# More expert matmuls ahead of a routing round's first comparison sums, from the third round on

## The chip, the cores and the metric

One core of a Trainium2 chip runs one program. The metric is the device time of that core in microseconds: 834.33 us before, the median of three runs (832.85 to 835.11).

## The reference

Attention over 4 x 8 heads of 576 positions feeds a dense layer pair, and that feeds a mixture of eight experts, in which tokens are assigned greedily, by falling logit, each expert taking at most 288 of 2304:

```python
x = attn_out ...                       # (2304, 512)
g = np.maximum(h, 0) + alpha * np.minimum(h, 0)   # h = x @ w_in
x = g @ w_out                          # (2304, 512)
logits = x @ w_gate                    # (2304, 8)
for idx in np.argsort(-logits.flatten()):
    tok, e = idx // 8, idx % 8
    if assigned[tok] >= 0 or counts[e] >= 288: continue
    assigned[tok] = e; counts[e] += 1
for e in range(8):
    out[mask_e] = np.maximum(x[mask_e] @ w1[e], 0) @ w2[e]
```

## The kernel before

The first 560 us are attention and the dense layers. The change concerns what follows: the routing and the eight experts, which run side by side.

**Routing.** It goes in eight rounds, p = 0 to 7; each finds the expert that fills up first, its 288 tokens, and closes it. In a round, DVE writes the best free expert of each token (`best`, L796 to L801), and `search` then brackets the threshold in four iterations (five in round 0). An iteration is a comparison on DVE (`against`, L912, two halves, tile `cmp`), 18 short matmuls on TensorE that sum it (L1088, tile `prt`; "the sums" below), a test on DVE (L1094, tile `ge`), two more short matmuls (L1097, L1098; "the step" below), and a new set of thresholds on DVE (L1100). Then `members` (two matmuls, L1165 and L1166, and DVE work) numbers the tokens, and `index` makes the list `ix` of their rows (18 matmuls, L1212, and DVE L1215). Round 7 has no search. POOL's queue gathers the rows (L1231, tile `xg`), and TensorE transposes them (L1266, `expert_x`), which ACT and DVE split into `exh` (L1270) and `exl` (L1271).

**An expert.** Expert p (the one that round p found) has 96 matmuls of the first layer (L1300, eight blocks f, 12 each, into `phx`), then 96 of the second (L1318, four columns c, 24 each, into `pyx`). After block f, ACT writes `hh` (L1306) and DVE `hl` (L1307); the second layer needs both of every block. ACT empties a column into `yt` (L1324), TensorE transposes it back after the next expert's first block (L1336), ACT writes `row` (L1344) and POOL's queue scatters it (L1347). A weight block is loaded by SP's queue (`wr`, L1243, three buffers), cast by ACT in two halves (`ws`, L1248), and its rest is taken by POOL in two subtractions (L1251), behind the gather of the same expert. There are two sets of `ws`, so the weights of expert p+1 are prepared while expert p runs.

**What sets the order.** TensorE's order is written out by a planner (the loop at the end of the kernel): `experts()` yields the expert's pieces with a cost in ns each (490 for four first-layer matmuls, 370 for three second-layer ones), `routing()` yields the delay until its next TensorE piece may stand in the order. When the planner's time `now` reaches `ready`, the routing piece is placed, else the next expert piece. `ahead(now)` places the gather and the weights of a round that has been numbered. The delay before an iteration's sums is `(LB if it == 0 else LU) + NB * K / 1.92` with LB = 1700. The other engines' order follows from the program order and a scheduler, and each engine runs its queue in order. So ACT, DVE and POOL each carry both routing and expert work in one line.

Of the kernel before, what the change touches and what calls it, by code (L numbers as in the profile page):

```python
# [25 lines left out]

LEAST = 896 * 16
KG = 15
FW = 20
ND, OG0, OGS, OG1 = 11, 48, 2, 125.5  # L30
WE = 1
# [16 lines left out]
LB, LU, LG, LM, LI, LX, LX1, L0 = 1700, 600, 400, 4300, 5600, 8000, 3000, 0  # L48
# [57 lines left out]
def attention_moe_kernel(ctx, tc, qt, kt, vt, wm, alpha, wg, we, out, NB=18, dbg=None):  # L106
# [81 lines left out]
    def w_scales():  # L188
# [19 lines left out]
        nc.vector.tensor_tensor(s[:, 0:1], to[:, 0:1], to[:, 2:], ALU.mult)  # L208
        nc.vector.tensor_scalar(s[:, 2:], back[:, 0:1], back[:, 1:2], 2.0 ** KG, op0=ALU.mult, op1=ALU.mult)
        nc.vector.tensor_tensor(s[:, 2:], s[:, 2:], e[:, 2:], ALU.mult)  # L210
# [50 lines left out]
    def small_loads():  # L261
# [8 lines left out]
        for a, b in zip(slope[0], scaled):  # L270
            nc.vector.tensor_scalar(b, a, 2.0 ** -KG, None, op0=ALU.mult)

# [414 lines left out]
    def fill(n):  # L687

        for _ in range(min(n, len(rest))):
            with tc.issue_after(LAST["pl"].ins):  # L690
                rest.pop(0)()
# [214 lines left out]
    def rows_of(ap):  # L906
        return ap[:, :, None].to_broadcast([P, ap.shape[1], J])

    def against(out, ramp, x, op):

        d = [P, out.shape[1], ramp.shape[1] // J, J]
        nc.vector.tensor_tensor(out.rearrange("p b (k j) -> p b k j", j=J),  # L912
                                ramp.rearrange("p (k j) -> p k j", j=J)[:, None].to_broadcast(d),
                                x[:, :, None, :].to_broadcast(d), op)
# [70 lines left out]
    def do(fn, *a):  # L985
        if LABEL is not None:
            LABEL.append((nc.get_next_instruction_name(), fn.__name__, [x for x in a if isinstance(x, int)]))
        fn(*a)
# [60 lines left out]
    def warm(n):  # L1049

        for _ in range(n):
            nc.tensor.matmul(idle[:, :2 * P], ones, ones[:, None, :].to_broadcast([P, 2, P]), start=True, stop=True)
# [5 lines left out]
    def search(p, scale):  # L1058

        r = R[p]  # L1060
        K, its, KL = (K1, I1, KL1) if p else (K0, I0, KL0)

        u16 = rt.tile([P, NB, J], F16, name="u16", bufs=3)
        nc.vector.tensor_scalar(u16, rows_of(r["m"]), scale[K], MID, op0=ALU.mult, op1=ALU.add)
        old = r["m"], scale[K], ALU.mult
        for it in range(its):
            last = it == its - 1
            if last:
                K = KL
            th = ramps["steps"][:, 64 - K // 2:64 + K // 2]  # L1070
            for cs in HALVES:
                against(cmp[:, cs, :K], th, u16[:, cs], ALU.is_le)
            if not last:

                by = K if it < its - 2 else KL // 2
                u, uk = u_, uk_[it % 2]
                nc.vector.tensor_scalar(u, old[0], old[1], 2.0 * K, op0=old[2], op1=ALU.min)
                nc.vector.tensor_scalar(uk, u, -2.0 * K, float(by), op0=ALU.max, op1=ALU.mult)
            if not p:
                fill(FILL[2 + it])  # L1080
            elif p == 1 and it == 0:
                warm(WP)

            yield (LB if it == 0 else LU) + NB * K / 1.92
            pr = psum.tile([P, 2, NE], F32, name="prt", bufs=PR)
            cnt, ne = pr[:, 0], pr[:, 1]
            for c in range(NB):
                nc.tensor.matmul(cnt, cmp[:, c], r["ob"][:, c], start=c == 0, stop=c == NB - 1)  # L1088
            if not p:
                fill(FG_)  # L1090
            ge = rt.tile([P, NE], F16, name="ge", bufs=2)
            if not last:
                g1 = rt.tile([P, 1], F16, name="g1", bufs=2)
                nc.vector.tensor_scalar(ge[:K], cnt[:K], float(CAP), None, op0=ALU.is_ge, op1=ALU.max,  # L1094
                                        accum_out=g1[:K])
                yield LG
                nc.tensor.matmul(ne[:, :1], times[by][:K], half[:K], start=True, stop=False)  # L1097
                nc.tensor.matmul(ne[:, :1], times[by][:K], g1[:K], start=False, stop=True)  # L1098
                u16 = rt.tile([P, NB, J], F16, name="u16", bufs=3)
                nc.vector.tensor_scalar(u16, rows_of(uk), ne[:, :1], MID, op0=ALU.subtract, op1=ALU.add)  # L1100

                ne_ = rt.tile([P, 1], F32, name="ne", bufs=2)
                nc.vector.tensor_copy(ne_, ne[:, :1])
                old = uk, ne_, ALU.subtract
            else:
                nc.vector.tensor_scalar(ge[:K], cnt[:K], float(CAP), None, op0=ALU.is_ge)
                yield LG
                nc.tensor.matmul(ne, ones[:K], ge[:K], start=True, stop=True)
                n = rt.tile([P, 1], F32, name="n", bufs=2)
                nc.vector.tensor_reduce(n, ne, axis=AX.X, op=ALU.max)  # L1110

                v = v_
                nc.vector.tensor_scalar(v, u16[:, :, 0], n, MID - K // 2, op0=ALU.subtract, op1=ALU.subtract)
        ev_ = rt.tile([P, NE], F32, name="ev", bufs=2)
        nc.vector.scalar_tensor_tensor(ev_, ne, 8.0, e_rev, op0=ALU.mult, op1=ALU.add)
        r["u"], r["pick"] = v, ev_
# [69 lines left out]
    def index(p):  # L1186
# [30 lines left out]
        if not p:  # L1217
            warm(FW)

# [150 lines left out]
    def routing():  # L1370
        for p in range(NE):
            for d in routing_(p):
                yield d * M1 if p == 1 else d
# [27 lines left out]
    def experts():  # L1401
        for _ in stepped(("expert_x", 0), (1 for _ in expert_x_(0))):
            yield 0, XC
        yield 0, 400
        for p in range(NE):
            for f in range(8):
                for c in stepped(("expert_1", p), (1 for _ in expert_1(p, f))):
                    yield 0, 490
                yield 0, 490
                if p > 1 and f == YF:  # L1410
                    for k in range(G3):
                        do(expert_y, p - 1, k)
                        yield 0, 450
            for c in range(4):
                if 0 < p < NE - 1 and c == XE:
                    while p + 1 not in gathered:
                        yield None, 0
                    yield gathered[p + 1], 1300
                    do(expert_x, p + 1)
                for _ in stepped(("expert_2", p), (1 for _ in expert_2(p, c))):  # L1420
                    yield 0, 370
                yield 0, 370
            if p == 0:
                while 1 not in gathered:
                    yield None, 0
                yield gathered[1], 1300
                do(expert_x, 1)
                for k in range(G3):
                    do(expert_y, 0, k)
                    yield 0, 450  # L1430
            current[0] = min(p + 1, NE - 1)
            if p == NE - 1:
                for k, half in (0, 0), (1, 0), (0, 1), (2, 0), (1, 1), (2, 1):
                    do(expert_y, p, k, half)

    def ahead(now):

        for p in sorted(placed - set(gathered)):
            if p <= current[0] + 1:
                with tc.high_priority(offset=HP):  # L1440
                    do(gather, p)
                gathered[p] = now + (LX if p > 1 else LX1)
        for p in sorted(picked):
            while loaded[p] < (8 if p in gathered else W0 if p else 0) and p <= current[0] + 1:
                do(expert_weights, p, loaded[p])
                loaded[p] += 1

    current = [0]
    route, work = routing(), experts()
# [3 lines left out]
    now = gathered[0] = LX1  # L1453
# [6 lines left out]
    w = next(work, None)  # L1460
    while w is not None or ready < INF:
        if ready <= now and len(placed) <= current[0] + 2 or w is None or w[0] is None:
            now = max(now, ready)
            with tc.high_priority(offset=HP):
                d = next(route, None)
            ready = INF if d is None else now + d
        elif w[0] <= now or ready == INF or len(placed) > current[0] + 2:
            now = max(now, w[0]) + w[1]
            w = next(work, None)
        else:  # L1470
            now = min(w[0], ready)
        ahead(now)
# [46 lines left out]
```

## Time and profile before

| | us |
|---|---|
| median of three runs | 834.33 |
| the profiled execution | 840.6 |
| its span, first to last instruction | 838.9 |
| busy: TensorE, DVE, ACT, POOL | 796.7, 578.8, 458.0, 281.5 |
| mean granted TensorE clock | 0.969 |

TensorE is busy for 95% of the span. The share says little by itself, because a matmul at the lower clock is longer and counts as busy too. The stretches to look at are those of single experts, from the first matmul of an expert to that of the next, with the clock of each and the waits inside it.

### The profile page before, as it was taken

The page shows a single profiled execution, that of the slowest core. Times are in us where ns is not written, and L with a number is a line of the kernel's source. Part 1 is how long each engine was busy: PE and PEld are TensorE (multiplying, and loading weights), DVE is VectorE, ACT ScalarE, POOL GpSimd, SP SyncE. Part 2 cuts the span into 40 slices and gives each one's busy share as a digit, 9 for nine tenths or more (in the row PEclk, how much of TensorE's full clock was granted, in tenths as well). Part 3 has the DMA queues.
Part 4 walks back from the last instruction along what each step waited for, and adds up shares of the span by engine and source line. Part 5 has one row for each costly group of instructions (what it writes and reads, how often), then busy time and mean ns, then how long its engine had stood idle before and what let it go on. Part 6 is the DMA issues. An engine that isn't in the chain of part 4 may idle for free.

```text
span 838.9 us, 18221 instructions
## 1 busy us (share of the span) xinstructions
PE 796.7 (95%) x6854; PEld 647.0 (77%) x6854; DVE 578.8 (69%) x1757; ACT 458.0 (55%) x1105; POOL 281.5 (34%) x256
## 2 busy tenths in 40 slices
PE   7789999999999999999999999989999979999996
PEld 5567776777777767777777777758999879999995
DVE  6996588988687777888868754786776666752120
ACT  4899367856555655655655544424546344455531
POOL 4344020101110010101100000019799875888921
PEclk7799999999999999999999999998999899999999
DMA  8997101114233142242411000034656554566500
GB/s 295 297 343 232 38 26 51 39 29 112 63 102 77 32 115 57 64 102 64 106 34 31 9 1 27 2 111 148 202 185 203 155 179 155 157 182 199 162 29 29
DMA packets 49144, 93.22 MB, mean 111 GB/s; under 512 B 22800, under 2 KB 22816, under 8 KB 49056
## 3 DMA queue, kind: packets, MB, share of 16 engines
q1 hardware_dynamic: 45984, 82.62, 33.1%
q0 software_dynamic: 3072, 9.44, 3.6%
q8 instruction: 54, 0.88, 0.4%
q14 instruction: 34, 0.28, 0.1%
HBM read 78.40 MB, written 9.44 MB: 105 GB/s over the span
## 4 chain that ended last, share of the span: by engine, by line
PE 80%; DVE 7%; DMA 5%; ACT 2%; issue 2%; POOL 1%; SPq 1%; another core or an unknown queue 0%; POOLq 0%; DVEq 0%; ACTq 0%
PE ph L705 22%; PE py L748 18%; PE pyx L1318 12%; PE phx L1300 11%; PE S L535 3%; PE py L740 2%; PE prt L1088 2%; PE pav L629 2%; DMA raw<-in_wm_dram 2%; PE pav L621 1%; PE pt L570 1%; DMA wr<-in_we_dram 1%; DVE wf L184 1%; PE pty L879 1%; PE pt L650 1%
## 5 line engine op out<-in xcount | busy, mean ns | idle before, releaser
L705 PE MATMUL ph<-xh,wp 128*128 128x256 f16 x1536 | 199.1, 273 | 0.3 <-DVE g L712 0.3
L705 PEld LDWEIGHTS <-wp 128*128 128x128 f16 x1536 | 147.6, 98 | 42.2 <-issue 1.6
L1251 POOL TENSOR_TENSOR ws<-wr,ws 128x512 fp32r<-128x512 f32 x128 | 160.4, 1287 | 13.7 <-ACT ws L1248 13.3
L436 POOL TENSOR_TENSOR ks<-kr,ks 64x512 fp32r<-64x512 f32 x34 | 51.2, 1511 | 282.3 <-ACT ks L435 271.0
L748 PE MATMUL py<-wp,gh 128*128 128x512 f16 x468 | 131.0, 380 | 0.3 <-ACT gh L730 0.3
L711 ACT ACTIVATE g<-ph,sg 128x256 f32<-128x256 f32 x144 | 67.5, 470 | 95.9 <-PE ph L705 94.7
L1318 PE MATMUL pyx<-hh,ws 128*128 128x288 f32 x512 | 111.0, 303 | 0.0
L1248 ACT ACTIVATE ws<-wr 128x512 fp32r<-128x512 f32 x128 | 73.2, 627 | 55.8 <-DMA wr<-in_we_dram 49.3
L712 DVE SCALAR_TENSOR_TENSOR g<-ph,sa,g 128x256 f32<-128x256 f32 x144 | 68.9, 478 | 42.7 <-ACT g L711 42.3
L1300 PE MATMUL phx<-exh,ws 128*128 128x288 f32 x512 | 88.2, 310 | 0.0
L1318 PEld LDWEIGHTS pyx<-hh,ws 128*128 128x128 f32 x512 | 85.5, 191 | 0.0
L748 PE MATMUL py<-wp,gl 128*128 128x512 f16 x234 | 78.2, 380 | 0.7 <-DVE gl L731 0.6
L1300 PEld LDWEIGHTS phx<-exh,ws 128*128 128x128 f32 x512 | 76.0, 197 | 0.8 <-ACT exh L1270 0.3
L1318 PE MATMUL pyx<-hl,ws 128*128 128x288 f32 x256 | 76.2, 298 | 0.0
L730 ACT ACTIVATE gh<-g 128x256 f16<-128x256 f32 x117 | 48.4, 413 | 44.6 <-DVE g L712 39.4
L748 PEld LDWEIGHTS <-gh 128*128 128x128 f16 x468 | 44.0, 98 | 31.4 <-issue 0.5
L1307 DVE SCALAR_TENSOR_TENSOR hl<-phx,hh 128x288 fp32r<-128x288 f32 x64 | 28.8, 455 | 52.6 <-ACT hh L1306 52.1
L731 DVE TENSOR_TENSOR gl<-g,gh 128x256 f16<-128x256 f32 x117 | 53.0, 453 | 15.6 <-ACT gh L730 15.4
L561 ACT ACTIVATE e<-e,mn 128x128 f32<-128x128 f32 x116 | 45.2, 392 | 11.0 <-DVE mn L558 10.8
L1318 PEld LDWEIGHTS pyx<-hl,ws 128*128 128x128 f32 x256 | 48.9, 191 | 0.0
L1300 PE MATMUL phx<-exl,ws 128*128 128x288 f32 x256 | 47.3, 308 | 0.0
L1306 ACT ACTIVATE hh<-phx 128x288 fp32r<-128x288 f32 x64 | 25.1, 404 | 39.2 <-PE phx L1300 27.2
(302 smaller groups left out, 1541.1 us busy)
## 6 DMA issues: line engine op xcount, KB each, us to landing
wr<-in_we_dram SPq DMA_DIRECT2D x64, 512.0 KB, 3.7
raw<-in_wm_dram SPq DMA_DIRECT2D x16, 1023.8 KB, 6.3
kr<-in_k_dram SPq DMA_DIRECT2D x68, 128.0 KB, 2.7
qr<-in_q_dram SPq DMA_DIRECT2D x64, 128.0 KB, 2.7
y_dram<-y SPq DMA_DIRECT2D x16, 256.0 KB, 2.0
vr<-in_v_dram SPq DMA_DIRECT2D x13, 256.0 KB, 2.6
whole<-in_v_dram SPq DMA_DIRECT2D x4, 256.0 KB, 6.6
whole<-in_q_dram SPq DMA_DIRECT2D x4, 128.0 KB, 2.5
```

The lines of the kernel that those rows point to most:

```text
L436: nc.gpsimd.tensor_sub(ks[64:], KR[n][64:], f32(ks[64:]))
L561: nc.scalar.activation(e[:, h], e[:, h], AF.Exp, bias=mn[:, h:h + 1], scale=-1.0, accum_out=SM[b][:, hh:hh + 1])
L705: LAST["l1"] = nc.tensor.matmul(ph, w[f][:, c * P:(c + 1) * P], x[u][:, c, :], start=i == 0, stop=i == 4 * len(pairs) - 1)
L711: KEPT[order.index((u, f))] = nc.scalar.activation(g, ph, AF.Copy, scale=sg)
L712: TURN[order.index((u, f))] = nc.vector.scalar_tensor_tensor(g, ph, sa, g, op0=ALU.mult, op1=ALU.max)
L730: nc.scalar.activation(gh, g, AF.Copy)
L731: nc.vector.tensor_sub(gl, g, gh)
L748: nc.tensor.matmul(PY[u][i], a[:, i * P:(i + 1) * P], w[f][:, 512:], start=f == 0 and j == 0, stop=f == FT - 1 and j == 2)
L1248: nc.scalar.activation(wh[s][:, h], w[:, h], AF.Copy)
L1251: (nc.vector if on_dve else nc.gpsimd).tensor_sub(wl[s][:, h], w[:, h], f32(wh[s][:, h]))
L1300: nc.tensor.matmul(ph, w[s][:, c * P:(c + 1) * P], x[:, c], start=i == 0, stop=i == 11)
L1318: nc.tensor.matmul(py, w[s][:, cs], r[x][f], start=i == 0, stop=i == 23)
```

## The change

The delay before the sums of a round's first iteration grows by DB = 2500 ns of the planner's time in rounds 2 to 7 (round 7 has no search). A second edit lets the expert work go on as soon as a gather is placed that it waited for in the planner; nothing else differs.

```diff
+DB = 2500
@@ search
-            yield (LB if it == 0 else LU) + NB * K / 1.92
+            yield (LB if it == 0 else LU) + NB * K / 1.92 + (DB if p > 1 and it == 0 else 0)
@@ planner loop, after a routing piece
             ready = INF if d is None else now + d
+            if w is not None and w[0] is None:
+                ahead(now)
+                w = next(work, None)
```

Lines behind the first edit move by one (L1088 is L1089 after), those behind the last by four.

TensorE, round 4, between the index matmuls of round 3 (L1212, tile `g`) and the sums of the first comparison (tile `cmp`). Before:

```order
L1212 LDWEIGHTS g
L1212 MATMUL prt<-col,g 128x6
L1300 MATMUL phx<-exl,ws_8833 128x288 x4
L1300 MATMUL phx<-exh,ws_8833 128x288 x4
L1300 MATMUL phx<-exh,ws_8840 128x288 x4
L1300 MATMUL phx<-exl,ws_8840 128x288 x4
L1300 MATMUL phx<-exh,ws_8840 128x288 x4
L1300 MATMUL phx<-exh,ws_8847 128x288 x4
L1088 LDWEIGHTS cmp
L1088 MATMUL prt<-ob,cmp 128x8
```

After, the last rows ahead of the same sums:

```order
L1319 MATMUL pyx<-hh_9314,ws_8858 128x288
L1319 MATMUL pyx<-hl_9315,ws_8858 128x288
L1319 MATMUL pyx<-hh_9314,ws_8858 128x288
L1319 MATMUL pyx<-hh_9331,ws_8865 128x288
L1319 MATMUL pyx<-hl_9332,ws_8865 128x288
L1319 MATMUL pyx<-hh_9331,ws_8865 128x288
L1089 LDWEIGHTS cmp
L1089 MATMUL prt<-ob,cmp 128x8
```

Before, 24 expert matmuls stood there, all of expert 2's first layer; now 45 stand there, all of its second layer. Rounds 2 and 3 go from 24 to 45 as well, round 5 from 24 to 44, round 6 from 23 and 12 transposes to 45; each round thus ends later in the expert work than before.

DVE, round 3, from the thresholds after the first step to the second test (`ge`). Before, `exl` of expert 2 stood an iteration later:

```order
L1100 TENSOR_SCALAR u_8923<-rs,prt 128x72
L1103 COPY ne<-prt 128x1
L912 TENSOR_TENSOR cmp<-rs,u_8923 128x1280
L912 TENSOR_TENSOR cmp<-rs,u_8923 128x1024
L1077 TENSOR_SCALAR rs<-rs,ne 128x18
L1078 TENSOR_SCALAR rs<-rs 128x18
L1094 TENSOR_SCALAR ge,g_8968<-prt 128x8
```

After:

```order
L1101 TENSOR_SCALAR u_8967<-rs,prt 128x72
L1104 COPY ne<-prt 128x1
L913 TENSOR_TENSOR cmp<-rs,u_8967 128x1280
L913 TENSOR_TENSOR cmp<-rs,u_8967 128x1024
L1272 TENSOR_TENSOR exl<-ptx,exh 128x288 x4
L1078 TENSOR_SCALAR rs<-rs,ne 128x18
L1095 TENSOR_SCALAR ge,g_9025<-prt 128x8
```

The four `exl` of the next expert now stand ahead of a test, in rounds 2, 3 and 4 alike.

ACT, first layer of expert 2 from its fourth block on (`ws` are the weights of expert 3). Before:

```order
L1306 ACTIVATE hh_9263<-phx 128x288
L1248 ACTIVATE ws_9323<-wr 128x512 x2
L1306 ACTIVATE hh_9280<-phx 128x288
L1306 ACTIVATE hh_9385<-phx 128x288
L1306 ACTIVATE hh_9402<-phx 128x288
L1248 ACTIVATE ws_9330<-wr 128x512 x2
L1306 ACTIVATE hh_9451<-phx 128x288
```

After:

```order
L1307 ACTIVATE hh_9237<-phx 128x288
L1307 ACTIVATE hh_9280<-phx 128x288
L1249 ACTIVATE ws_9190<-wr 128x512 x2
L1307 ACTIVATE hh_9297<-phx 128x288
L1249 ACTIVATE ws_9366<-wr 128x512 x2
L1307 ACTIVATE hh_9314<-phx 128x288
L1249 ACTIVATE ws_9373<-wr 128x512 x2
L1307 ACTIVATE hh_9331<-phx 128x288
```

The third weight block of expert 3 was cast ahead of the fifth `hh`; now it is cast ahead of the last. In experts 3 and 4 even the fourth block of the next weights stands ahead of the last `hh`.

## Rows read from the trace of the kernel before

**Rows 1.** Stages, TensorE: stretch, us, busy (instructions), granted clock, DMA share, GB/s

```profile
638.26:674.47 36.21, 34.45 (x317) 0.91 0.52 158
674.47:713.79 39.32, 35.03 (x337) 0.91 0.54 173
713.79:745.80 32.01, 31.53 (x318) 1.00 0.60 175
...
774.48:802.49 28.01, 28.01 (x218) 1.00 0.43 130
```

**Rows 2.** Waits of TensorE, 560 to 838 us: total us, times, longest

```profile
PE prt L1088 <- DVE cmp L912: 5.2, 3, 3.5
PE prt L1097 <- DVE ge L1094: 2.3, 3, 1.2
```

**Rows 3.** Timeline, TensorE: start, us, work, [idle before, releaser]

```profile
653.54 0.41 PE L1088 MATMUL prt<-ob,cmp 128*128 128x8 f16 x10 [1.54 <-DVE cmp L912]
...
686.87 0.41 PE L1088 MATMUL prt<-ob,cmp 128*128 128x8 f16 x10 [3.45 <-DVE cmp L912]
```

**Rows 4.** Stages: us, PE, PEld, DVE, ACT, POOL busy, granted clock, DMA

```profile
653.00:661.00 8.00, 7.24 (x61) 6.80 (x62) 4.50 (x16) 1.56 (x3) 7.67 (x8) 0.57 0.52 144
```

**Rows 5.** Chain of waits: start, us, what; expert matmuls at either clock

```profile
657.07 2.88 PE pyx L1318 x12
...
816.60 12.67 PE pyx L1318 x96
```

**Rows 6.** Chain of waits, up to the first wait of rows 3

```profile
643.50 5.34 DMA wr<-in_we_dram
...
649.99 0.40 ACT hh L1306
...
650.41 0.46 DVE hl L1307
...
652.75 0.74 DVE cmp L912
```

**Rows 7.** Timeline, ACT, ahead of the second wait

```profile
680.99 0.41 ACT L1306 ACTIVATE hh<-phx 128x288 fp32r<-128x288 f32 x1
685.18 0.41 ACT L1306 ACTIVATE hh<-phx 128x288 fp32r<-128x288 f32 x1 [3.78 <-remote]
```

**Rows 8.** Timeline, DVE: a later comparison, and three `exl`

```profile
635.01 1.26 DVE L1271 TENSOR_TENSOR exl<-ptx,exh 128x288 fp32r<-128x288 f32 x3
...
661.99 1.42 DVE L912 TENSOR_TENSOR cmp<-rs,u 128x1280 f16<-128x1280 f16 x2
```

**Rows 9.** Timeline, TensorE: a step, the sums after it, the transposes of gathered rows

```profile
661.42 0.18 PE L1097 MATMUL prt<-half,times 128*128 128x1 f16 x1
...
663.53 0.61 PE L1088 MATMUL prt<-ob,cmp 128*128 128x8 f16 x18
...
670.09 1.15 PE L1266 MATMUL ptx<-ident,xg 96*128 96x96 f32 x12
671.03 0.38 PE L1318 MATMUL pyx<-hh,ws 128*128 128x288 f32 x1
```

**Rows 10.** Timeline, TensorE: two shorter waits

```profile
239.80 0.20 PE L629 MATMUL pav<-vp,et 128*128 128x64 f16 x1 [0.96 <-DVE et L608]
...
567.14 0.16 PE L1097 MATMUL prt<-half,times 128*128 128x1 f16 x1 [1.25 <-DVE ge L1094]
```

**Rows 11.** Stages, TensorE: the clock behind those two

```profile
240.00:242.00 2.00, 1.58 (x28) 1.00 0.00 0
...
570.00:575.00 5.00, 4.98 (x35) 0.50 0.65 198
```

**Rows 12.** Timeline, ACT: a cast that waits for its load

```profile
653.71 1.15 ACT L1248 ACTIVATE ws<-wr 128x512 fp32r<-128x512 f32 x2 [1.79 <-DMA wr<-in_we_dram]
```

**Rows 13.** The tile `wr`, 600 to 760 us: POOL's subtraction (ns); load time

```profile
L1251 POOL TENSOR_TENSOR ws<-wr,ws x86: 1262/1286/1317, 598.8 to 759.9; 128x512 fp32r<-128x512 f32 x86
...
DMA to landing us min/median/max: 3.6/3.7/5.1
```

**Rows 14.** Timeline, POOL and TensorE: last gather issue of expert 0, first use

```profile
566.04 0.92 POOL L1231 DMA_INDIRECT xg<-y_dram,ix  x1 [0.30 <-issue]
...
569.25 0.90 PE L1284 MATMUL ptx<-ident,xg 96*128 96x96 f32 x4 [0.30 <-DMA xg<-y_dram,ix]
```

## Prediction

> **What bounds the kernel now.** I read the stages first, cut at the first matmul of each expert. Expert 6 has no routing beside it and takes 28.01 us at full clock; expert 4, with four sums, a `members` and an `index`, takes 32.01 us, also at full clock. Experts 2 and 3 carry about the same routing and take 36.21 and 39.32 us, at a mean clock of 0.91 [rows 1]. So TensorE sets the pace here, and the two slow experts are where something can be had. Expert 2 has one `members` more than expert 4 (0.1 us) and expert 3 one `index` more (0.5 us, about what 18 such short matmuls take). What they lose is 36.21 - 32.01 - 0.1 = 4.1 us and 39.32 - 32.01 - 0.5 = 6.8 us, together **10.9 us**.
>
> The waits of TensorE say at what: 5.2 us in three waits for a comparison, and less for tests [rows 2]. The timeline puts two of the three, 5.0 us, at 653.5 us (1.54 us, round 4) and 686.9 us (3.45 us, round 5), both at the first comparison of a round [rows 3], where the change puts more work. The rest of the loss is the clock: 0.57 granted over the 8 us from 653 [rows 4], which is (1 - 0.57) / 0.5 x 8 = 6.9 us at 1.2 instead of 2.4 GHz. An expert matmul goes at 2.88 / 12 = 0.24 us there and at 12.67 / 96 = 0.132 us at full clock [rows 5]. A stretch after a wait thus costs 4.1 - 1.5 = 2.6 us by the span of expert 2, and 6.9 x (1 - 0.132 / 0.24) = 3.1 us by the pitch of the matmuls; I use 2.6.
>
> The chain of waits tells why the comparison was late. A weight load took 5.34 us, the cast behind it waited, `hh` stood behind the cast on ACT, `hl` behind `hh`, and the comparison behind `hl` on DVE [rows 6]. For the second wait the same `hl` and comparison stood behind an `hh` that started 3.78 us after ACT was free, and the profile names no engine that released it [rows 7].
>
> **What the change removes.** Between the `members` matmuls of a round and the next round's first sums, 72 expert matmuls and the `index` stood in round 4, and 92 stand now: 20 x 0.132 = 2.6 us more, where DVE was 1.5 us late. In round 5 it was 61 matmuls and 12 transposes (1.2 us), and it is 92: 31 x 0.132 - 1.2 = 2.9 us more, where DVE was 3.5 us late. By count alone wait one goes and 0.6 us of wait two stays. But in round 4 the comparison no longer has the late `hh` near it: the last block of the first layer is three matmuls ahead of the `index`, and 45 matmuls follow. In round 5 the last `hl` stands ahead of the comparison, yet 36 matmuls (4.8 us) lie between its block and the sums. I take both waits and both clock stretches as gone: **-10.9 us**. Rounds 2, 3 and 6 had no wait there beyond the 0.2 us left over in [rows 2], and gain nothing. The added work is no new work: the same matmuls stand elsewhere later, and as TensorE has work of the experts to the end, the later rounds cost nothing by themselves. The second edit of the planner moves no row by itself, since the expert work never has to ask for rows not yet gathered.
>
> **What it adds.** Three places.
>
> First, the test behind the four `exl` in rounds 2, 3 and 4. From a step on, DVE's comparison ends after 661.99 + 1.42 - 661.42 = 2.0 us; four `exl` take 4 x 1.26 / 3 = 1.7 us at most [rows 8], less their overlap, say 1.5, and the test 0.25: 3.75 us. TensorE does in that time, in round 3, transposes (0.94 us), three matmuls (0.4), the sums (some 0.5, since the next start overlaps their end) and six matmuls (0.8) [rows 5, 9], 2.65 us. It waits 1.1 us; in round 2 the transposes of `yt` give the same sum, 1.1 us; in round 4 six matmuls more stand there, 0.8 us, and 0.3 us is left. Sum **+2.5 us**; bounds: 0, if `exl` finds a gap earlier, and 3.5.
>
> Second, the last `hh` and `hl` of experts 3 and 4. ACT has the cast of the fourth weight block of the next expert ahead of the last `hh`. That load needs a `wr` buffer, which POOL frees after the first block's two subtractions (2 x 1.29 us), and the load takes 3.7 us, at most 5.1 [rows 13]. The first block's cast stands behind the fourth `hh` (the third in expert 4), so the fourth cast ends about 1.2 + 2.6 + 3.7 + 1.2 = 8.7 us behind that, while four blocks and an `index` take 4 x 1.6 + 0.5 = 6.9 us on TensorE (five blocks in expert 4). The last `hh` is then 1.8 us late in expert 3 and in time in expert 4. The second layer wants the last `hl` 21 matmuls (2.8 us) behind its block, of which `hh` and `hl` take 1.2 of ACT and DVE: 1.6 us of lateness are free. So by the median load the wait is 0.2 us and 0, by the longest one 1.6 us and 0, and POOL has three scatters to issue as well and may be 2 us later still. Bounds 0 and 2 us per expert (a cast here waited 1.79 us for its load [rows 12]); I take **+1.0 us** for the two.
>
> Third, the clock. A wait of 0.96 us left it at 1.00, one of 1.25 us was followed by 0.50 [rows 10, 11]. The 1.1 us waits lie between the two; I count one stretch in all, **+2.6 us** (bounds none and three, 0 to 7.8). The Trainium skill, TensorE: Matmul & The Clock Gate, section Terms, counts time at the half rate as half lost. By that page the 6.9 us would cost 3.4 us, where the matmul rows show 3.1 and the span 2.6, and the forecast would come out 0.8 us later.
>
> The gather of expert 2 also comes closer to its use: 69 matmuls and three sums stood between, now 51 and one. That is 51 x 0.132 + 0.5 = 7.2 us. The gather has three issues 0.92 + 0.30 us apart, and the last landed at most 569.25 - 566.04 = 3.2 us after its start [rows 14]: 5.6 us, which leaves 1.6 us for DVE's list and the start on POOL. No term.
>
> **Sum.** -10.9 + 2.5 + 1.0 + 2.6 = -4.8 us. Against its own time the profiled execution would go from 840.6 to 835.8. That execution is 6.3 us above the median of 834.33. I assume that the timed runs have the two waits too and take the same difference: **829.5 us**.
>
> **Rivals.** *The second wait is not in the timed runs.* Its 6.8 us are close to the 6.3 us by which the profiled execution is longer, and it hangs on one wait of ACT without a named releaser [rows 7]; against it, the first 80 us could hold the surplus as well. Then 4.1 us go and 6.1 come: 836.3; with no clock stretch among the new waits 833.7. Both lie within 0.3% (2.5 us) of before, which is about what a measurement of this kernel can tell from no change. *The new waits are hidden.* DVE finds `exl` ready earlier and the weights come in time: 834.3 - 10.9 = 823.4; for it, four rounds of before had no such wait; against it, the order rows. *The weights become the bound, and it is slower.* POOL's subtractions wait for the gather, the gather for the later round; each expert needs 16 x 1.29 + 6 x 1.22 = 28 us of POOL within some 31 us. If POOL's first subtraction for the next expert comes 2 us later than reckoned, behind the scatters, the last `hl` of experts 3, 4 and 5 makes TensorE wait about 1.5 us and each wait draws a clock stretch: 3 x (1.5 + 2.6) = 12.3 us on top of the 2.5, against 10.9: 838.2. It decides where these waits pass the 1 us that left the clock alone. *The change does not do what it says* is ruled out by the order: the sums stand later in every round.
>
> **How the numbers follow.** The forecast, 826 to 831.8, has 0.40; the hidden waits, below 826, 0.15; the change that nobody can tell, 831.8 to 836.8, 0.30; slower 0.15. So faster 0.55, same 0.30, slower 0.15. The range leaves out half of the case below 826 and half of the slower one: 823.5 to 837.5; the likeliest case alone is 826 to 832.
>
> **What would show it.** Right: no wait for L912 above 0.5 us in rounds 4 and 5, experts 2 and 3 at full clock or with one stretch, and the step of rounds 2 and 3 about 1 us behind a test. Wrong: expert matmuls of the second layer waiting for `hl`, TensorE waiting for `xg` at expert 2, or spans of experts 2 to 5 that sum to what they did.

## The result and the profile after

The changed kernel takes 839.23 us (median of 14 runs, 834.40 to 844.44) where the kernel before takes 832.64 us beside it (14 runs, 828.19 to 836.80): a ratio of 1.0088, with a 95% interval of 1.0064 to 1.0112 (the quotient of the two medians is 1.0079). Forecast were 829.5 us and a range of 823.5 to 837.5; the change is slower by less than 1.2%, and the time lies above the range. Two later groups of runs, on two chips, give 1.0030 (1.0002 to 1.0058) and 1.0004 (0.9976 to 1.0032); that difference between groups bears on the explanation. Here and below, a figure like 1.0030 is the time as a multiple of that of the kernel before in the same group, with its 95% interval behind it.

The waits of TensorE from 560 to 839 us in the profile after (total us, times, longest), which answer to [rows 2]:

```profile
PE prt L1098 <- DVE ge L1095: 3.4, 5, 1.3
PE prt L1166 <- DVE ss L1153: 2.5, 1, 2.5
PE ptx L1285 <- DMA xg<-y_dram,ix: 2.4, 3, 1.6
PE prt L1213 <- DVE col L1203: 2.3, 2, 1.4
PE pox L1337 <- ACT yt L1325: 1.5, 1, 1.5
PE prt L1089 <- DVE cmp L913: 0.4, 2, 0.2
PE pyx L1319 <- ACT hh L1307: 0.3, 1, 0.3
```

The waits for the first comparison did go, from 5.2 to 0.4 us. In their place TensorE waits for the numbering (`ss`), longer for the index list (`col`; before had one such wait of 1.5 us, ahead of expert 0), for more tests, and in the last expert for `yt`. The 2.4 us for gathered rows (`xg`) are those of expert 0, ahead of the changed rounds; a second profile of before has 2.6 us there. The stages of experts 1, 2, 3 and 7 after (stretch, us, busy, granted clock, DMA share, GB/s), which answer to [rows 1]:

```profile
604.11:639.84 35.73, 32.65 (x324) 0.95 0.54 163
639.84:673.65 33.81, 31.76 (x323) 1.00 0.58 172
673.65:710.17 36.52, 33.93 (x336) 0.95 0.50 162
...
801.15:839.40 38.25, 28.52 (x218) 0.92 0.14 43
```

Against the profiled execution of before, experts 2 and 3 are 5 us shorter, about half of the 10.9 us forecast, while experts 1 and 7 are 3 and 2 us longer. But that execution (840.6 us) lay above each of the 14 timed runs of before.

How a late cast reaches the list is to be read in expert 2 of the profile after, on four engines (start, us, what, [idle before, releaser]):

```profile
653.41 1.15 ACT L1249 ACTIVATE ws<-wr 128x512 fp32r<-128x512 f32 x2 [2.61 <-DMA wr<-in_we_dram]
654.47 0.39 ACT L1307 ACTIVATE hh<-phx 128x288 fp32r<-128x288 f32 x1
...
654.90 0.46 DVE L1308 SCALAR_TENSOR_TENSOR hl<-phx,hh 128x288 fp32r<-128x288 f32 x1 [1.86 <-ACT hh L1307]
...
656.61 0.26 DVE L1203 TENSOR_TENSOR col<-rs,ids 128x108 f16<-128x108 f32 x1
...
656.92 0.59 PE L1213 MATMUL prt<-col,g 128*128 128x6 f16 x18 [1.37 <-DVE col L1203]
...
658.86 0.94 POOL L1232 DMA_INDIRECT xg<-y_dram,ix  x1 [2.20 <-DVE ix L1216]
```

The cast of the next expert's first block waits for its load (2.61 us); `hh` stands behind the cast, `hl` behind `hh`, the list (`col`) behind `hl`, the index matmuls behind the list, and the gather behind those; POOL stands idle for the last 2.20 us ahead of it.

### The profile page after: what moved, and what is told of

Its sections match the earlier page's. It is cut to its first block, busy times and chain, and to the rows that moved or that the text cites. A ratio compares the mean times of both kernels' runs of the same rounds, so it can differ in the third digit from the quotient of the medians.

```text
span 839.4 us, 18217 instructions
## 1 busy us (share of the span) xinstructions
PE 793.5 (95%) x6854; PEld 643.9 (77%) x6854; DVE 579.8 (69%) x1757; ACT 457.3 (54%) x1105; POOL 280.5 (33%) x256
## 3 DMA queue, kind: packets, MB, share of 16 engines
q1 hardware_dynamic: 45984, 82.62, 32.8%
## 4 chain that ended last, share of the span: by engine, by line
PE 69%; DVE 12%; DMA 7%; POOL 4%; ACT 4%; issue 3%; SPq 1%; POOLq 0%; ACTq 0%; DVEq 0%
PE ph L706 20%; PE py L749 16%; PE pyx L1319 9%; PE phx L1301 8%; DMA wr<-in_we_dram 4%; PE S L536 3%; PE py L741 2%; POOL ws L1252 2%; PE pav L622 2%; PE pav L630 2%; PE pt L571 1%; DVE wf L184 1%; PE prt L1089 1%; ACT ws L1249 1%; DMA vr<-in_v_dram 1%
## 5 line engine op out<-in xcount | busy, mean ns | idle before, releaser
L1249 ACT ACTIVATE ws<-wr 128x512 fp32r<-128x512 f32 x128 | 73.8, 625 | 75.5 <-DMA wr<-in_we_dram 69.0
```

Source lines behind the costliest of these rows:

```text
L1249: nc.scalar.activation(wh[s][:, h], w[:, h], AF.Copy)
```

## The experiments

Three theories were weighed. **Theory 0**: the gain was hardly there to be had, since most executions of before don't have both waits of [rows 3]. **Theory 1**: the rounds come later, so the gathers and the weights of the next expert come later, and ACT's casts wait for loads ahead of `hh`, `exh` and `yt`. **Theory 2**: the tests behind the four `exl` cost the time. All kernels compute the whole result. The runs came in five groups, each on one chip with the kernel before beside it; the second and the fifth group ran on the same chip. Each kernel was profiled once in its group.

### First group (before: 831.17 us)

The kernel before, profiled again.

> The kernel before, profiled once more. Theory 0 (the gain was not there to be had): the two waits of TensorE for the first comparison, 1.54 us in round 4 and 3.45 us in round 5, belong to the one profiled execution; a second one shows at most one of them, experts 2 and 3 together take about 70 us instead of 75.5, and the time is near 832. Rival (the waits are in every run): both are there again with 5.0 us together, and the span is near 838.

It took 829.04 us. Its stages of experts 1 to 3, and its waits for the first comparison:

```profile
604.75:636.53 31.78, 31.24 (x323) 1.00 0.71 197
636.53:668.72 32.19, 31.86 (x320) 1.00 0.58 181
668.72:702.07 33.35, 32.36 (x336) 1.00 0.67 203
```

```profile
PE prt L1088 <- DVE cmp L912: 1.1, 6, 0.2
```

Neither of the two waits is there, and experts 2 and 3 take 65.5 us at full clock where the execution I predicted from took 75.5. Some 10 us of the forecast's gain, 10.9 us, are missing in this one.

`exl` behind the test, with TensorE's order as in the changed kernel:

```diff
-            nc.vector.tensor_sub(xl[:, c], pts[c], f32(xh[:, c]))
...
+        def rests():                        # called some matmuls later, experts 1 to 7
+            with tc.issue_after(LAST["ge"].ins):
+                for c in range(4):
+                    nc.vector.tensor_sub(xl[:, c], pts[c], f32(xh[:, c]))
```

> The changed kernel with one edit: the four exl of the next expert are queued on DVE behind the test (ge) of the iteration they stood ahead of. TensorE's order is that of the changed kernel, row for row. Theory 2 (the tests behind exl cost the time): the step's waits for ge of 0.68, 0.43, 0.69 and 1.31 us go, with them a half-clock stretch, and the time falls by 3 to 6 us to 833 to 836. Theory 1 (the weights come later, and casts that wait for them hold hh, exh and yt on ACT): it falls by 1 us at most, 838 to 839.

It took 846.18 us, 1.0192 (1.0150 to 1.0234). Its waits from 600 us on:

```profile
PE prt L1214 <- DVE col L1204: 5.0, 3, 3.4
PE prt L1090 <- DVE cmp L914: 2.1, 3, 1.7
PE pox L1346 <- ACT yt L1334: 1.4, 1, 1.4
PE prt L1099 <- DVE ge L1096: 0.8, 1, 0.8
```

The waits for `ge` mostly went as meant (0.8 us in one), and the ratio is higher still than that of the changed kernel, which ran in another group. So taking these waits away by this edit does not give the time back, and theory 2 is not borne out. It is not excluded either: the edit brings other waits, 3.4 us for `col` and 1.7 us for a comparison, and what the waits for tests cost by themselves was not run.

The delay in half of the rounds:

```diff
-            yield ... + (DB if p > 1 and it == 0 else 0)
+            yield ... + (DB if p in (4, 5) and it == 0 else 0)      # db_45
+            yield ... + (DB if p in (2, 3, 6) and it == 0 else 0)   # db_236
```

> The changed kernel with the added delay in rounds 4 and 5 alone, the two rounds whose first comparison was waited for. If the loss comes from rounds 2 and 3 (a test behind exl, a late load in expert 1): no slower than before, 829 to 833. By theory 1 every shifted round delays a gather and with it the weights: about half of the loss stays, 835 to 837.

> The changed kernel with the added delay in rounds 2, 3 and 6 alone, the other half. If the loss comes from rounds 2 and 3: as slow as the changed kernel, 838 to 841. By theory 1: about half of the loss, 835 to 837.

db_45 took 832.01 us, 1.0014 (0.9988 to 1.0040), db_236 835.91 us, 1.0066 (1.0038 to 1.0094). Where the profile of before has no wait in rounds 4 and 5, the delay there gains nothing and costs nothing that the interval shows; most of the loss comes from the other three rounds. Theory 1, as I had put it, wanted half from each.

### Second group (before: 837.53 us): the weights

```diff
-        w = ex.tile([P, 1024], F32, name="wr", bufs=3)
+        w = ex.tile([P, 1024], F32, name="wr", bufs=4)   # wr4, wr4_db0; 2 in wr2_db0
...
-            t = rt.tile([P, NB, NE], F32, name="t", bufs=2)
+            t = rt.tile([P, NB, NE], F32, name="t", bufs=1)  # wr4, wr4_db0: for room
...
-W0 = 1
+W0 = 3                                                   # w0_3
```

> The changed kernel with four wr buffers in place of three (and one buffer of t in place of two, for room). TensorE's order is that of the changed kernel, row for row; nothing else is meant to move but the start of the weight loads. Theory 1 (lateness of the weights: casts that wait for a load hold hh, exh and yt on ACT, hl and the index list on DVE, and so the gather, behind which the next subtractions stand): the casts' waits for loads ahead of hh shrink, the waits of TensorE for col, ss and ge (6 us) mostly go, and the time falls by 4 to 8 us to 831 to 835. Rival (the later rounds are the loss by themselves: work moved to where there is no cover): within 1.5 us of the changed kernel.

> The kernel before with the same four wr buffers (and one buffer of t). Theory 1: before has slack enough, its subtractions end 30 to 33 us into an expert of 32; it gains little, 0 to 3 us, 828 to 832, and its two waits for the first comparison do not come up. Rival: a gain as large as in the changed kernel.

> The changed kernel with three weight blocks, not one, placed as soon as a round has picked its expert (W0 = 3). TensorE's order is unchanged. POOL then takes six subtractions instead of two to four ahead of the gather, in the time in which it waited 2.2 to 4.6 us for the list. Theory 1: the weights are ready some 4 us sooner in experts 2 to 6 and the time falls by 3 to 7 us, 832 to 836. Rival: within 1.5 us of the changed kernel, or slower, since the gather now stands behind six subtractions.

> The kernel before with two wr buffers: its sums stand where they stood, the weights alone come later. Theory 1: the waits of the changed kernel appear (TensorE for col, ss, ge, cmp, yt, each of 1 us and more), several with the clock at 0.5 behind them, and it is slower than the changed kernel, 842 to 870. Rival: the loads are hidden anyway, under 835.

wr4 took 836.18 us, 0.9967 (0.9936 to 0.9997); wr4_db0 841.41 us, 1.0050 (1.0021 to 1.0078); w0_3 845.53 us, 1.0078 (1.0029 to 1.0127); wr2_db0 847.82 us, one run. The changed kernel was not in this group; beside wr4's second run, in the third group, it is the slower one. So a fourth load buffer helps the changed kernel, and against what I expected it harms the kernel before. wr4 and wr4_db0 also give up one of two buffers of `t`, a tile of the numbering on DVE, and no run separates the two edits. With two load buffers the transposes of `yt` wait in before too, as in the changed kernel, though the largest wait is another, for `ws` itself, and the waits for `col` and `ss` that theory 1 expected did not come (waits of wr2_db0, 570 to 840 us):

```profile
PE phx L1300 <- ACT ws L1248: 4.2, 4, 2.7
PE pox L1336 <- ACT yt L1324: 2.5, 2, 1.7
```

w0_3 went against theory 1 as I had worded it, and the way that its rival had named: the gather stands behind six subtractions on POOL. In expert 1 its first issue starts at 632.22 us, right behind them, and TensorE waits for the rows at 638.50; it waits for tests as well (waits of w0_3, 600 to 720 us, and its expert 1):

```profile
PE prt L1098 <- DVE ge L1095: 7.7, 7, 1.6
PE ptx L1267 <- DMA xg<-y_dram,ix: 2.6, 5, 1.6
```

```profile
607.00:647.53 40.53, 35.61 (x325) 0.87 0.46 145
```

Weights that are asked for sooner do not help by themselves; it matters what stands in line behind them.

### Third group (before: 838.07 us): the changed kernel beside its parts

> The changed kernel once more, as the reference of this group. 1.005 to 1.012 times the kernel before. If the waits of its first profile are the rule and not one execution's: index matmuls waiting for col, steps waiting for ge, the last transposes of yt 1.5 us late, and at least one half-clock stretch in experts 1 to 3. Rival (as with the kernel before, the profile was one execution's): a different set of waits at the same time.

> The changed kernel with four wr buffers, beside the changed kernel on the same chip. Theory 1 (late weights are the loss): 0.8 to 1.4% below the changed kernel, and at or below the kernel before, 0.993 to 1.000. Rival (the first comparison of the two was of two chips): within 0.3% of the changed kernel.

> The changed kernel with the added delay in rounds 2 and 3 alone. Theory 1: the lists of experts 2 and on come later by what two delays add, the first casts of each expert meet loads that are not there: 1.003 to 1.006 times the kernel before. Rival (the loss of rounds 2, 3 and 6 is the late yt in round 6): 0.998 to 1.002.

> The changed kernel with the added delay in round 6 alone. Theory 1: no earlier list is late, so the weights of expert 7 have their slack and the cost is 0 to 1.5 us: 0.998 to 1.002. Rival: the transposes of yt wait 1.5 us and the round costs that by itself, 1.002 to 1.005.

after_again took 841.41 us, 1.0030 (1.0002 to 1.0058), less than the 1.005 to 1.012 expected; wr4_again 837.08 us, 0.9990 (0.9968 to 1.0012), 0.4% below it, half of what was expected; db_23 843.80 us, 1.0073 (1.0049 to 1.0098); db_6 837.11 us, 0.9990 (0.9967 to 1.0013). Rounds 2 and 3 alone seem to cost more here than the whole change, though the two intervals overlap. That would mean that rounds 4 and 5 give something back on this chip. db_6, whose order up to round 5 is that of before, shows what: its expert 3, and the same of after_again, with the stall of ACT in after_again:

```profile
673.63:712.64 39.01, 35.02 (x335) 0.91 0.56 175
```

```profile
675.72:710.94 35.22, 32.53 (x336) 1.00 0.52 165
```

```profile
685.88 0.41 ACT L1307 ACTIVATE hh<-phx 128x288 fp32r<-128x288 f32 x1 [2.83 <-remote]
```

In db_6 the wait of [rows 3] is back (3.50 us, with the lower clock behind it). In after_again ACT stands still in the same way, 2.83 us without a named releaser as in [rows 7], but no comparison's sums stand close behind, and TensorE loses 0.2 us on them; the index matmuls behind it wait 1.1 us for `col`. There the change does what it was forecast to do. The profile of db_23 has no such stall in expert 3 (32.8 us), but two shorter ones in expert 4 (2.00 and 1.09 us), which takes 38.1 us.

Experts 1, 2 and 7 of wr4_again, and the same of after_again, tell where the fourth buffer helps:

```profile
602.73:634.59 31.86, 31.12 (x325) 1.00 0.59 183
634.59:668.15 33.56, 32.22 (x324) 1.00 0.53 172
...
796.22:832.90 36.68, 28.46 (x218) 0.94 0.11 33
```

```profile
606.75:640.14 33.39, 31.33 (x324) 1.00 0.57 172
640.14:675.72 35.58, 33.27 (x324) 0.95 0.56 169
...
801.62:840.20 38.58, 28.52 (x218) 0.95 0.14 43
```

In experts 1 and 2 `hl` waits for `hh` 4.8 us in db_6, 10.7 in after_again, 7.7 in wr4_again (the waits of DVE in those two stages, in this order):

```profile
DVE hl L1308 <- ACT hh L1307: 4.8, 6, 1.9
```

```profile
DVE hl L1308 <- ACT hh L1307: 10.7, 9, 2.8
```

```profile
DVE hl L1308 <- ACT hh L1307: 7.7, 12, 2.0
```

The waits of the casts on ACT in the same two stages, db_6 first, then after_again:

```profile
ACT ws L1249 <- DMA wr<-in_we_dram: 16.5, 14, 2.8
...
ACT ws L1249 <- POOL ws L1252: 0.6, 1, 0.6
```

```profile
ACT ws L1249 <- DMA wr<-in_we_dram: 16.6, 10, 3.6
...
ACT ws L1249 <- POOL ws L1252: 4.6, 2, 3.1
ACT ws L1249 <- issue: 3.9, 1, 3.9
```

The time for which casts wait for loads is the same; what comes on top in after_again is the wait for POOL and one of 3.9 us without a releaser. With those, casts wait 17.6 us in db_6, 25.1 in after_again and 18.3 in wr4_again.

### Fourth and fifth group (before: 836.93 and 837.70 us): two questions left

One link of the chain is taken out: DVE's list work goes ahead of the `hl` of later blocks.

```diff
-            nc.vector.tensor_tensor(ss[:, 1], s0, ss[:, 0], ALU.subtract)
+            LAST["list"] = nc.vector.tensor_tensor(ss[:, 1], s0, ss[:, 0], ALU.subtract)
...
-        nc.vector.tensor_tensor(col, ...)
+        LAST["list"] = nc.vector.tensor_tensor(col, ...)
...
+        with tc.issue_after(LAST["list"].ins):
             nc.vector.scalar_tensor_tensor(hl, ph, 0.0, f32(hh), op0=ALU.max, op1=ALU.subtract)
```

> The changed kernel with DVE's list work (ss in members, col in index) queued ahead of the hl of blocks written behind it; TensorE's order is unchanged, and the weights are as late as before. If the loss runs over the list (cast waits for its load, hh behind the cast, hl behind hh, col behind hl): the waits of the index matmuls for col and of members for ss (3 to 5 us with the half-clock stretches behind them) go, the gathers come 1 to 2 us sooner, and the time falls to 0.995 to 1.002 times the kernel before, 3 to 6 us below the changed kernel. If late weights reach TensorE mostly by other ways (hl of the second layer, yt, exh): 1 us at most, 1.004 to 1.009.

> The added delay in rounds 4 and 5 alone, once more. If the kernel before has the long wait for the first comparison in round 5 on this chip (its median near 838, and the look at it shows the wait): the delay removes it with its half-clock stretch, 0.992 to 0.998. If the kernel before does not have it here (median near 831): 0.999 to 1.004 as at first.

> The delay in rounds 4 and 5 alone, with four wr buffers (one buffer of t). If the gain of rounds 4 and 5 and that of the earlier loads add: 0.990 to 0.997 times the kernel before. If the fourth buffer helps only where rounds 2 and 3 are late too: 0.998 to 1.005, as with the kernel before and four buffers.

> The kernel before, a third profile, on the chip of this group. On a chip where its median is near 838: a wait of about 3.5 us of round 5's first comparison behind an hh that no row explains, with the clock at 0.5 behind it, and expert 3 at 38 to 39 us. On a chip where it is near 831: no such wait, and expert 3 at 33 to 34 us.

before_look took 834.21 us and has the second wait again, with the stall of ACT ahead of it:

```profile
680.22 0.41 ACT L1306 ACTIVATE hh<-phx 128x288 fp32r<-128x288 f32 x1 [3.54 <-remote]
...
681.91 0.41 PE L1088 MATMUL prt<-ob,cmp 128*128 128x8 f16 x10 [3.18 <-DVE cmp L912]
```

On this chip db_45_again takes 833.94 us, 0.9975 (0.9951 to 0.9999), a gain that its interval barely clears, and wr4_45 834.50 us, 0.9964 (0.9937 to 0.9992). That the delay in rounds 4 and 5 gains where before has the stall fits what was expected; with one profile of before in each of the two groups it is not shown. The profile of db_45_again takes expert 3 from 37.8 to 32.7 us, but its expert 4 takes 37.2 us in place of 32.0: TensorE waits 1.9 us there for the first comparison of round 6. The two gains do not visibly add. Both take a little less than before here (the changed kernel did not run in this group); with 1.0014 in the first group, db_45 is no version that is faster everywhere. list_first took 838.14 us, 1.0017 (0.9993 to 1.0041); beside the changed kernel on one chip:

> The changed kernel, beside list_pair on one chip: 1.002 to 1.009 times the kernel before; the higher, the lower the median of before is on this chip (near 831: 1.007 to 1.010; near 837: 1.002 to 1.005).

> The changed kernel with the list work ahead of hl, beside after_pair. If the list carries most of the loss of rounds 2 and 3 (5 to 6 us): 0.4 to 0.7% below after_pair. If it carries little of it: within 0.2% of after_pair, with the waits moved to ge, hl and exl.

after_pair took 837.12 us, 1.0004 (0.9976 to 1.0032), again below what was expected; list_pair 839.21 us, 1.0018 (0.9995 to 1.0041). Their waits from 600 us on, after_pair first:

```profile
PE prt L1213 <- DVE col L1203: 4.0, 3, 2.1
PE prt L1098 <- DVE ge L1095: 2.5, 3, 1.4
PE pox L1337 <- ACT yt L1325: 1.3, 1, 1.3
```

```profile
PE prt L1098 <- DVE ge L1095: 4.0, 4, 1.7
PE pyx L1320 <- ACT hh L1307: 1.8, 1, 1.8
PE pox L1338 <- ACT yt L1326: 1.1, 1, 1.1
PE prt L1109 <- DVE ge L1107: 1.0, 1, 1.0
```

The 4.0 us for the list are gone, the time is not: about as much has come up elsewhere, at tests and at `hh`. The list is where the lateness showed; taking the wait for it away by this edit, which holds `hl` back in turn, does not give the time back.

## Why the prediction was wrong, step by step

The spans of the stages put the account together (us, cut at the first matmul of each expert; most cuts of [rows 1] lie 0.2 us later):

| kernel | experts 0 + 5 | 1 + 2 | 3 | 4 | 6 | 7 |
|---|---|---|---|---|---|---|
| before, first profile | 64.25 | 68.73 | 39.16 | 32.01 | 28.00 | 36.58 |
| before_again, no stall | 63.71 | 63.97 | 33.35 | 32.25 | 27.94 | 36.53 |
| before_look, stall | 63.32 | 65.70 | 37.80 | 31.97 | 27.80 | 36.53 |
| db_6, stall | 63.80 | 65.35 | 39.01 | 33.39 | 27.83 | 36.53 |
| changed, first profile | 64.25 | 69.54 | 36.52 | 32.54 | 28.57 | 38.25 |
| after_again | 63.27 | 68.97 | 35.22 | 32.82 | 28.00 | 38.58 |
| after_pair | 63.47 | 67.83 | 34.91 | 32.56 | 27.80 | 38.12 |
| wr4_again | 65.72 | 65.42 | 33.31 | 34.24 | 29.52 | 36.68 |

**The gain of 10.9 us: the step that failed first.** "I assume that the timed runs have the two waits too" does not hold, as far as profiles tell. The first wait, with its clock stretch 4.1 us by the forecast, came up in none of before_again, before_look and db_6: experts 1 and 2 together take 64 to 66 us there, against 68.73 in the execution I read. The second, 6.8 us by the forecast, hangs on a stall of ACT that is there in some profiles and not in others. Where it is, the change takes expert 3 from 39.0 us (db_6) to 35.2 (after_again, on the same chip), 3.8 us. Where it isn't, expert 3 goes from 33.35 (before_again) to 36.52 in the first profile after. My first rival had this condition, for the second wait alone, and its 833.7 to 836.3 were still too low, for the next step.

The signs that were to show it right came true all the same: no wait for the first comparison above 0.5 us, experts 2 and 3 with one stage below full clock, steps 0.4 to 0.7 us behind a test. Experts 2 to 5 took 132.7 us in the first profile after, against 136.2 in the one I read from. These signs asked what became of one execution, and left out experts 1 and 7, which are longer.

**Late `hh` and `hl`, +1.0 us: the right lateness, the wrong reader, and too small.** I priced lateness by the second layer, which wants the last `hl`; in the first profile after it waited 0.3 us for `hh`. I did not ask what else stands behind `hl` on DVE: the numbering and the list. And I reckoned with experts 3 and 4, where it sets in with expert 1. Measured, experts 1 and 2 go from 65.4 (db_6) to 69.0 us (after_again), 3.6 us: TensorE stands idle 2.4 us longer, with 3.4 us of waits for `col` that db_6 does not have and less for tests and comparisons, and its busy time is 1.2 us longer, with the clock of expert 2 at 0.95. The 2.5 us for `ss` in the first profile came with one load of 7.8 us and is 0.2 us in after_again. That the cause lies with casts that wait is supported by wr4_again: with a fourth load buffer casts wait 18.3 us in place of 25.1, and experts 1 and 2 are back at 65.4. It is not shown by itself, since wr4 moves other instructions of ACT and DVE as well and takes a buffer from `t`; and experts 4 and 6 are 1.4 and 1.5 us longer in it than in after_again. That it all runs over the list was my next guess, and list_pair did not bear it out. By which of the many ways it runs stays open.

**"The later rounds cost nothing by themselves": wrong at the end.** Expert 7 takes 38.1 to 38.6 us in place of 36.5. In the profile after its weights are still being prepared when it starts:

```profile
803.20 1.15 ACT L1249 ACTIVATE ws<-wr 128x512 fp32r<-128x512 f32 x2 [1.63 <-POOL ws L1252]
804.26 0.39 ACT L1325 ACTIVATE yt<-pyx 128x288 f32<-128x288 f32 x1
...
804.70 1.19 PE L1337 MATMUL pox<-ident,yt 128*96 128x128 f32 x9 [1.46 <-ACT yt L1325]
```

The cast waits for POOL (in after_again, for its load), `yt` for the cast, the transposes for `yt`: 1.5 us that no later stage gives back. db_6 has none of it, with 36.5 us for expert 7, nor have db_45 (36.6) and db_23 (36.5): the delay of round 6 alone does not do it, nor do those of earlier rounds alone. In db_236 the same wait of 1.5 us comes one expert sooner. That fits theory 1.

**Tests behind `exl`, +2.5 us: about right as a wait, its price open.** The profile after has 0.68, 0.43 and 0.69 us in rounds 2 to 4, 1.8 in all, and 1.31 in round 5, behind one `exl`, which the forecast did not have. exl_late removes most of these waits and is no faster, but it brings others.

**The clock, one stretch, +2.6 us: about right.** after_again and after_pair have one stage below full clock between experts 1 and 5, the first profile two. Expert 3 of db_6 has a mean clock of 0.91 over 39.01 us, which is (1 - 0.91) / 0.5 x 39.01 = 7.0 us at 1.2 GHz in place of 2.4. TensorE's busy time in it is 35.02 - 32.36 = 2.7 us longer than in before_again at full clock, and the forecast took 2.6. The Trainium skill (TensorE: Matmul & The Clock Gate, section Terms) counts time at the half rate as half lost. By that, an estimate, the 7.0 us would cost 3.5, and the 2.7 measured here are less.

**The gather, no term: right.** TensorE does not wait for `xg` at expert 2 in the first profile after.

**The sum, made again.** From db_6 to after_again on one chip: -0.5 (experts 0 and 5), +3.6, -3.8, -0.6, +0.2, +2.0, and 0.4 before the experts: 1.3 us, which is the difference of their spans, 838.9 and 840.2. From before_again to the first profile after, neither of which has the stall: +0.5, +5.6, +3.2, +0.3, +0.6, +1.7 and 0.2: 12.1 us, again that of the spans (827.3 and 839.4); the medians differ by less, 6.6 us, since one execution lies low and the other high. Without the gain, the terms that the forecast added, 6.1 us, come close to these 6.6. That is luck: they were reckoned for the second layer's `hl` and for rounds 2 to 4, and what was measured stands in experts 1 and 2, at the list, and in expert 7. The third rival, weights that become the bound (838.2 us), had late weights and nearly the time, and got 0.15. Its time is luck as well: it takes off the 10.9 us and adds waits of the second layer in experts 3 to 5, of which the first profile after has 0.3 us.

## What to carry to other kernels

A wait that one profiled execution shows is worth its time only if other executions have it too: where that execution lies above every timed run beside it, first suspect that its largest waits are the surplus, and profile it again. Moving one step later moves what is queued behind it as well: follow each engine's line to its next steps (here cast, `hh`, `hl`, list, gather, next weights), not only to the first reader of a tile. A wait taken away at one link came up at the next; more slack at the source (a fourth load buffer) helped the changed kernel where reordering the links did not, and cost the kernel before 0.5%.

## What the runs showed of the hardware that I had not expected

ACT stood idle for 2.8 to 3.9 us ahead of an `hh` of expert 3 in the first profile of before, before_look, db_6, wr4_db0 and after_again, though the matmuls it reads had ended by the trace; the profile names no engine for it. Shorter ones, of 1.1 to 2.0 us, stand in expert 4 of db_23 and wr4_db0. None of the first group's four profiles has one, but neither have nine others of the later groups, nor the first profile after. The median of the kernel before is 837 to 838 us on the chips of those groups and 831 on that of the first, which fits a stall that goes with the chip. It is not shown: the first profile of before has the stall although the runs beside it have a median of 834.33 us, and before_look has it at 834.21 us, below the median of its group. What stalls ACT is open: no row shows it, and nothing was run to provoke it.

A 512 KB load took 3.4 to 4.5 us at the median of every profile from 600 to 760 us, but up to 8.3 us in the first profile after and 4.1 at most in after_again.
